# Three pieces later: when a pre-norm attention and MLP kernel loads and squares its other weights

## The chip, the cores and the metric

The kernel runs on one core of a Trainium2 chip. The metric is the device time of one execution in microseconds (us). Before the change the median of three runs is 1648.96 us (1647.39 to 1649.14).

## The reference, cut to what matters

```python
h  = x + softmax_attention(layernorm(x) @ wqkv) @ wo      # 2048 rows, 512 columns, 32 heads of 16
h2 = h + silu(layernorm(h) @ w1) @ w2                     # 512 -> 1792 -> 512
```

All arrays are float32. `wqkv` is 512 x 1536, `wo` 512 x 512, `w1` 512 x 1792 and `w2` 1792 x 512. The reference has no sum of squares of a weight. The kernel needs one for each weight, because it scales weights by powers of two that come from their norms before it splits them into two 16-bit parts.

## The kernel before, in words

**Stages.** The program first computes the first four value tiles and starts the projections (about the first 106 us), goes on with the Q and K projections of the other head groups (to about 200 us), and then runs attention, with the output projection and the MLP of each block of 512 rows woven in. Every engine works off its instructions in program order. SP issues all DMAs, in program order too, so a DMA that has to wait holds up all the DMAs behind it.

**The units of the projections.** The rows come in four blocks (`b` = 0 to 3). The loop at L648 to L691 goes over the blocks, and in a block over units: the K unit and the Q unit of the first head group (`n` = 0, 1, `project_qk`, L521), and, for b = 1 to 3, four V units (`n` = 2 to 5, `project_v`, L545). Unit (b, n) is counted as u = 0, 1 for block 0 and u = 2 + 6(b - 1) + n after it (L654). So (1, 2) is u = 4 and (1, 5) is u = 7. The loop at L716 to L733 follows with three head groups of eight K and Q units, u = 20 to 43; there `n` counts from -4 to 19, with u = n + 24.

**What a unit issues around the change.** A unit begins with `square_rest(u)` (L464). It squares one piece and asks for another:

```python
n = u - 4
if 0 <= n < len(pieces):
    act("activation", staged[n % 2], staged[n % 2], AF.Square, accum_out=rest_sq[:, n:n + 1])
n = u - 2
if 0 <= n < len(pieces):
    dma(staged[n % 2], pieces[n])
```

A piece is 128 x 512 float32, 256 KB, of `w1` (14 of them), `w2` (14) or `wo` (4). Two buffers, `staged`, hold them; both lie in `ks[4]`, so the profile names such a DMA `ks<-in_B_w_dram` (`ks<-in_A_wo_dram` for `wo`) and the square `ks<-ks`. The square is an instruction of ScalarE (ACT), and stands in ACT's order ahead of what the unit itself wants from ACT: the copy of the value tile out of PSUM (`va<-ps_v`, L550), the scaled copy of Q or K (`ks<-ps_qk` and `sh<-ks`, L534 and L535, into `scaled`, also in `ks[4]`), and the copy of turned rows (`xth<-ps_tr`, L209). A DMA into a buffer waits for the square that read it.

A K or Q unit of block 1 or later also has layer-norm work ahead of its product (`stats` and `norm`, by the tables at L645 to L647), GpSimd (POOL) makes the low part `sl`, and two DMAs store the result in `kd` or `qd`. After a Q unit eight DMAs load the block's K rows for the first two attention items (`ks<-kd`, L677; in block 0 eight of Q come with them). After (1, 0) the rows of block 3 are loaded, 1 MB (`load_x(3)`, L689, `ks<-in_A_x_dram`); after (1, 2) and (1, 4) four DMAs each write constant rows (`fixed_rows`, L235, `qs<-fix_q` and `ks<-fix_k`). Row maxima of the scores are woven into the units (`burst`, L393): a matmul into `ps_m`, of which there are five PSUM buffers, and a reduce on VectorE (DVE), `mx<-ps_m`. Products, value tiles and turned rows share three PSUM buffers (`st`). `split_qk` (L500) cuts the next Q or K weights in two: a cast on ACT, a subtraction on DVE, or on POOL in V units; for (1, 5) that is weight 3.

**The values' weights.** `square_values` (L460) squares the raw values' weights, 128 x 2048 elements, in one ACT instruction, and writes the squares over all of `ks[4]`, where nothing reads them. It is issued at L637, after the squares of the Q and K weights and ahead of the copies of the value tiles 1 to 3.

**What uses the sums.** `measure_rest` (L473, called for n = 14) adds the sums up over the partitions with a matmul (`ps_sq`), and `set_factors` (L483, called for n = 16) derives the factors on DVE and POOL. The attention stage uses them.

Of the kernel before, what the change touches and what calls it, by code (L numbers as in the profile page):

```python
# [88 lines left out]
def attention_mlp_kernel(ctx: ExitStack, tc: tile.TileContext, x, wqkv, wo, w1, w2, out):  # L89
# [5 lines left out]
    def mm(*a, **k):  # L95
        tc.keep_in_program_order(nc.tensor.matmul(*a, **k))  # L96
# [12 lines left out]
    def act(fn, *a, **k):  # L109
        pin(getattr(nc.scalar, fn)(*a, **k))  # L110
# [4 lines left out]
    def dma(*a):  # L115
        pin(nc.sync.dma_start(*a))
# [73 lines left out]
    def statistics(rows, scale=1.0):  # L190

        st = small.tile([P, 6], F32, name="st", bufs=5)
        mv = small.tile([P, 2], F32, name="mv", bufs=5)
        rs = small.tile([P, 1], F32, name="rs", bufs=5)
        dve("bn_stats", st, rows)
        dve("bn_aggr", mv, st)
        pool("tensor_scalar", rs, mv[:, 1:2], EPS, scale ** -2, op0=ALU.add, op1=ALU.mult)
        pool("tensor_tensor", rs, rs, expo, ALU.pow)
        return mv, rs

    def normalize(dst, rows, mv, rs, engine="dve"):
        (pool if engine == "pool" else dve)("tensor_scalar", dst, rows, mv[:, 0:1], rs, op0=ALU.subtract, op1=ALU.mult)

    def turn(src, dst_h, dst_l, kind="st"):

        ps = bank("ps_tr", kind).rearrange("p (c n) -> p c n", n=P)
        for c in range(4):
            tr(ps[:, c, :], src[:, c * P:(c + 1) * P], ident)
        act("copy", dst_h, ps)  # L209
        low(dst_l, ps, dst_h)  # L210
# [13 lines left out]
    def load_k(i, k, lo=0, n=S):  # L224
        a, j = HEADS[k]
        h = 4 * (i % 8) + 2 * a + j
        dma(ks[i % RING][64 * j:64 * j + 48, a, lo:lo + n], rows_of_head(kd, h)[:, lo:lo + n])

    def load_q(i, k):
        a, j = HEADS[k]  # L230
        h = 4 * (i % 8) + 2 * a + j
        lo = i // 8 * 512
        dma(qs[i % RING][64 * j:64 * j + 48, a, :], rows_of_head(qd, h)[:, lo:lo + 512])
# [101 lines left out]
    def tick():  # L335
        at["step"] += 1
        for step in [step for step in late if step < at["step"]]:

            finish_rest()
            for i in late.pop(step):  # L340
                place_max(i)
        for fn, a in agenda.pop(at["step"], ()):
            fn(*a)
# [82 lines left out]
    with ExitStack() as pa:  # L426
# [20 lines left out]
        def load_x(b, parts=1):  # L447
            n = 4 // parts
            for t in range(0, 4, n):
                r0 = b * 512 + t * P  # L450
                dma(xts[b][:, t:t + n, :], x[r0:r0 + n * P, :].rearrange("(t p) d -> p t d", p=P))
# [8 lines left out]
        def square_values():  # L460
            act("activation", ks[RING - 1].rearrange("p a n -> p (a n)").bitcast(F32).rearrange(
                "p (c n) -> p c n", n=512), raw_v, AF.Square, accum_out=rest_sq[:, sum(PIECES):])

        def square_rest(u):  # L464

            n = u - 4
            if 0 <= n < len(pieces):
                act("activation", staged[n % 2], staged[n % 2], AF.Square, accum_out=rest_sq[:, n:n + 1])
            n = u - 2
            if 0 <= n < len(pieces):  # L470
                dma(staged[n % 2], pieces[n])

# [21 lines left out]
        def square(n):  # L494
            g, key = divmod(n, 2)
            act("activation", qs[RING - 1].rearrange("p a n -> p (a n)").bitcast(F32).rearrange(
                "p (c n) -> p c n", n=P), raw_qk[key][:, :, g * P:(g + 1) * P],
                AF.Square, accum_out=sq[:, n:n + 1])
# [46 lines left out]
        def project_v(b, t):  # L545
            ps = bank("ps_v")
            weave(product(ps, lambda c: xth[b][:, c, t * P:(t + 1) * P], lambda c: xtl[b][:, c, t * P:(t + 1) * P],
                          lambda c: wv_h[:, c, :], lambda c: wv_l[:, c, :], DC),
                  {k: (lambda n=n: burst(n)) for k, n in BESIDE_V1.items()} if (b, t) == (1, 1) else {})
            act("copy", va[:, 4 * b + t, :, 0:DH], ps.rearrange("p (h d) -> p h d", d=DH))  # L550

        def turn_x(b, t):

            turn(xts[b][:, t, :], xth[b][:, :, t * P:(t + 1) * P], xtl[b][:, :, t * P:(t + 1) * P],
                 "sm" if b == 1 else "st")
# [10 lines left out]
        def columns(t):  # L566
            return slice(t * P, (t + 1) * P)
# [6 lines left out]
        def turn_high(b, t):  # L574
            ps = bank("ps_tr", "sm").rearrange("p (c n) -> p c n", n=P)
            for c in range(4):
                tr(ps[:, c, :], xts[b][:, t, c * P:(c + 1) * P], ident)
            act("copy", xth[b][:, :, columns(t)], ps)
            return ps
# [48 lines left out]
        for t in range(4):  # L628
            for c in range(DC):
                mm(ps_vs[t], xth[0][:, c, columns(t)], wv_l[:, c, :], start=False, stop=False)  # L630
                mm(ps_vs[t], xtl[0][:, c, columns(t)], wv_h[:, c, :], start=False, stop=c == DC - 1)
            act("copy", va[:, t, :, 0:DH], ps_vs[t].rearrange("p (h d) -> p h d", d=DH))
            if t == 0:
                load_x(2)
                for n in (*keys[3:], *range(0, NG, 2)):
                    square(n)
                square_values()  # L637
        turned = [turn_high(1, t) for t in range(2)]
        measure(lambda: normalize(xts[1][:, 3, :], xts[1][:, 3, :], *found.pop(3)))
        for t in range(2):  # L640
# [7 lines left out]
        for b in range(NB):  # L648
            units = [("qk", 1), ("qk", 0)]
            vs = [("v", t) for t in range(4)]  # L650
            found = {}
            for n, (kind, k) in enumerate(units + vs if b else units):
                tick()
                square_rest(2 + 6 * (b - 1) + n if b else n)  # L654
                rows, (stats, norm, turns) = None, ((), (), ())
                if b + 1 < NB:
                    rows = xts[b + 1]
                    stats, norm, turns = (other_ln if b else first_ln)[n]

                def layer_norm():  # L660
                    for t in stats:
                        found[t] = statistics(rows[:, t, :])
                    for t in norm:
                        normalize(rows[:, t, :], rows[:, t, :], *found.pop(t), engine="pool" if kind == "v" else "dve")

                if kind == "v":
                    project_v(b, k)
                else:

                    layer_norm()  # L670
                    project_qk(b, k, scale=b > 0)
                    if k == 0:
                        for i in range(2):
                            for h in range(4):
                                if b == 0:
                                    load_q(i, h)
                                load_k(i, h, b * 512, 512)  # L677
                if b:

                    n_max = BESIDE_V[b - 1][kind == "v"][n - 2 if kind == "v" else n]  # L680
                    burst(n_max, *[bank("ps_m")] * (n_max > 5))
                if kind == "v":
                    layer_norm()
                for t in turns:
                    turn_x(b + 1, t)
                if (b, n) in splits:
                    split_qk(splits.pop((b, n)), "pool" if kind == "v" else "dve")
                if b == 1 and n == 0:
                    load_x(3)  # L689
                if b == 1 and n in (2, 4):  # L690
                    fixed_rows(n // 2 - 1)  # L691
# [24 lines left out]
        for g in range(1, NG // 2):  # L716
            for m, (b, key) in enumerate([(b, 1) for b in range(NB)] + [(b, 0) for b in range(NB)]):
                tick()
                if g == 1 and m < 2:
                    fixed_rows(2 + m)  # L720
                n = 8 * g + m - 12
                square_rest(n + 24)
                if n == 14:
                    measure_rest()
                if n == 16:
                    set_factors()
                beside = {BESIDE_A1[m]: 6} if g == 1 and m < len(BESIDE_A1) else BESIDE_A
                if n >= 18:
                    beside = BESIDE_T[n - 18]
                project_qk(b, 2 * g + key, beside, True, "su" if n % 2 else "st")  # L730
                for load, i, h in loads.get(n, ()):
                    load(i, h)
# [443 lines left out]
    for g in range(groups):  # L1176
# [15 lines left out]
        if i in FIRSTS:  # L1192
            b, n = i // 8 - 1, c - OUTPUT
# [23 lines left out]
        n = maxima(g)  # L1217
# [61 lines left out]
```

## Time and profile before

| | us |
|---|---|
| median of three runs | 1648.96 |
| the profiled execution's own time | 1649.26 |
| its span in the trace | 1647.5 |
| PE busy in the span | 1624.0 (99%) |
| DVE busy | 1439.0 (87%) |
| ACT busy | 1206.6 (73%) |
| POOL busy | 363.5 (22%) |

The profile is of one execution. Its times count from the start of the span. PE is TensorE (PEld its weight loads), DVE VectorE, ACT ScalarE, POOL GpSimd and SP the engine that issues the DMAs. A row of the timeline gives start, duration, engine, line, operation, output and input, and in brackets how long the engine had been idle and what ended that. A row of the chain gives start, duration and what the end of the program waited for at that time. A row of the waits gives the total, the number of times and the longest. A row of the windows gives PE, PEld, DVE, ACT and POOL busy time, and behind them the granted clock of PE (1.00 is full speed), the DMA engines' share and GB/s. L96, L110, L113, L103 and L116 are the helpers for matmuls, ACT, DVE, POOL and SP.

### The profile page before, as it was taken

How to read it: one execution, taken by the hardware profiler on the slowest of the kernel's cores; microseconds unless marked ns; L12 is line 12 of the kernel's file. 1: busy time of each engine (PE TensorE's matmuls, PEld its weight loads, DVE VectorE, ACT ScalarE, POOL GpSimd, SP SyncE). 2: the span in 40 equal slices, each digit the busy share in tenths (PEclk: the TensorE clock that was granted, in tenths of full speed). 3: DMA queues.
4: the chain of work that ended last, by engine and by line, in shares of the span. 5: the costliest groups of instructions: out<-in, count | busy, mean ns of one | idle time of the engine just before them, and what ended most of it. 6: DMA issues, size and time to landing. Idle time of an engine off the chain costs nothing.

```text
span 1647.5 us, 28474 instructions
## 1 busy us (share of the span) xinstructions
PE 1624.0 (99%) x10553; PEld 516.1 (31%) x10553; DVE 1439.0 (87%) x2385; ACT 1206.6 (73%) x2391; POOL 363.5 (22%) x594
## 2 busy tenths in 40 slices
PE   9899999999999999999999999999999999999999
PEld 7566522222223322222223322222233322222254
DVE  7799999999999989999999989999988969999431
ACT  5445599999972169999972169999972179999732
POOL 4323354544421001121121001121121001111100
PEclk9999999999999999999999999999999999999999
DMA  5657344333432211111232211112132211100222
GB/s 192 170 142 220 100 96 121 99 107 107 117 76 85 71 51 32 34 36 49 54 76 85 70 51 32 33 36 53 51 77 90 65 50 32 36 12 21 72 81 73
DMA packets 100951, 125.91 MB, mean 76 GB/s; under 512 B 24144, under 2 KB 61072, under 8 KB 100812
## 3 DMA queue, kind: packets, MB, share of 16 engines
q1 hardware_dynamic: 100812, 124.10, 27.1%
q8 instruction: 82, 1.34, 0.3%
q14 instruction: 57, 0.47, 0.1%
HBM read 93.45 MB, written 24.63 MB: 72 GB/s over the span
## 4 chain that ended last, share of the span: by engine, by line
PE 79%; DVE 14%; ACT 4%; DMA 2%; issue 1%; POOL 0%; SPq 0%; DVEq 0%; ACTq 0%
PE pv L96 32%; PE ps_s L96 21%; DVE mx L271 11%; PE ps_m L96 10%; PE ps_qk L96 5%; PE ps_acc L96 4%; PE ps_w L96 3%; ACT pt L110 3%; PE ps_wo L96 2%; PE ps_v L96 2%; DVE gh L113 1%; DMA ks<-in_B_w_dram 1%; PE ps_tr L99 1%; DVE ot L113 0%; DVE pvs L113 0%
## 5 line engine op out<-in xcount | busy, mean ns | idle before, releaser
L271 DVE TENSOR_REDUCE mx<-ps_m 128x1 f32<-128x512 f32 x2011 | 1260.5, 683 | 68.1 <-PE ps_m L96 36.4
L110 ACT ACTIVATE pt<-ps_s 128x512 f32<-128x512 f32 x2048 | 1010.4, 608 | 30.0 <-PE ps_m L96 17.8
L96 PE MATMUL pv<-pt,va 128*17 128x512 f32 x4096 | 537.6, 598 | 0.9
L96 PE MATMUL ps_s<-qs,ks 64*128 64x512 f16 x2048 | 532.6, 379 | 2.0 <-ACT pt L110 0.5
L96 PE MATMUL ps_m<-ks,qs 48*128 48x512 f16 x2011 | 513.6, 381 | 9.0 <-DVE mx L271 6.1
L96 PEld LDWEIGHTS <-ks 64*128 64x128 f16 x2048 | 150.3, 95 | 550.0 <-issue 437.1
L110 ACT ACTIVATE g<-pv,factors 128x512 f32<-128x512 f32 x39 | 26.8, 688 | 217.5 <-PE pv L96 217.5
L96 PE MATMUL ps_acc<-w,gh 128*128 128x512 f16 x672 | 161.2, 380 | 0.0
L103 POOL TENSOR_TENSOR ri<-rc,minus 128x16 f32<-128x16 f32 x31 | 90.9, 2932 | 282.0 <-DMA rc<-dn 282.0
L96 PEld LDWEIGHTS <-qs 48*128 48x128 f16 x2048 | 119.6, 94 | 76.1 <-issue 70.1
L96 PEld LDWEIGHTS pv<-pt,va 128*17 128x17 f32 x4096 | 69.0, 95 | 215.3 <-issue 202.7
L103 POOL TENSOR_TENSOR mx<-mx 128x32 f32<-128x32 f32 x34 | 8.6, 254 | 403.5 <-DVE mx L271 402.0
L113 DVE SCALAR_TENSOR_TENSOR gh<-g,factors,gh 128x512 f16<-128x512 f32 x56 | 41.7, 745 | 63.7 <-ACT gh L110 63.7
L96 PEld LDWEIGHTS <-w 128*128 128x128 f16 x708 | 65.2, 98 | 93.6 <-issue 29.1
L96 PE MATMUL pv<-hth,w 128*128 128x512 f16 x312 | 92.9, 379 | 0.0
L96 PEld LDWEIGHTS <-gh 128*128 128x128 f16 x672 | 59.2, 98 | 95.1 <-issue 32.4
L110 ACT ACTIVATE ks<-ps_qk,qk_s 128x512 f32<-128x512 f32 x30 | 20.7, 689 | 53.3 <-PE ps_qk L96 45.7
L96 PE MATMUL pv<-htl,w 128*128 128x512 f16 x156 | 59.5, 381 | 0.0
L103 POOL TENSOR_SCALAR nm<-nm 128x16 f32<-128x16 f32 (+1 forms) x50 | 13.1, 261 | 198.7 <-DVE nm L282 195.7
L96 PE MATMUL ps_qk<-xth,wqk_h 128*128 128x512 f32 x128 | 53.6, 419 | 0.6 <-ACT va L110 0.6
L96 PE MATMUL ps_qk<-xth,wqk_l 128*128 128x512 f32 x128 | 50.7, 396 | 0.0
L103 POOL TENSOR_TENSOR sl<-ks,sh 128x512 f16<-128x512 f32 x30 | 34.8, 1161 | 70.4 <-ACT sh L110 56.9
(134 smaller groups left out, 1002.8 us busy)
## 6 DMA issues: line engine op xcount, KB each, us to landing
ks<-kd SPq DMA_DIRECT2D x120, 192.0 KB
w<-w1d SPq DMA_DIRECT2D x56, 256.0 KB
w<-w2d SPq DMA_DIRECT2D x56, 256.0 KB
ks<-in_B_w_dram SPq DMA_DIRECT2D x28, 256.0 KB
w<-in_B_w_dram SPq DMA_DIRECT2D x28, 256.0 KB
qs<-qd SPq DMA_DIRECT2D x128, 48.0 KB
kd<-sh SPq DMA_DIRECT2D x16, 256.0 KB
qd<-sh SPq DMA_DIRECT2D x16, 256.0 KB
```

Of the source, the lines that this page charges most:

```text
L96: tc.keep_in_program_order(nc.tensor.matmul(*a, **k))
L99: tc.keep_in_program_order(nc.tensor.transpose(*a))
L103: tc.keep_in_program_order(getattr(nc.gpsimd, op)(*a, **k))
L110: pin(getattr(nc.scalar, fn)(*a, **k))
L113: pin(getattr(nc.vector, fn)(*a, **k))
L271: pin(nc.vector.tensor_reduce(mx[piece][:, j, a % n, qt, kb:kb + 1], ps, axis=AX.X, op=ALU.max))
```

## The change

```diff
         def square_rest(u):
-            n = u - 4
+            n = u - 7
             if 0 <= n < len(pieces):
                 act("activation", staged[n % 2], staged[n % 2], AF.Square, accum_out=rest_sq[:, n:n + 1])
-            n = u - 2
+            n = u - 5
             if 0 <= n < len(pieces):
                 dma(staged[n % 2], pieces[n])
...
                 for n in (*keys[3:], *range(0, NG, 2)):
                     square(n)
-                square_values()
...
                 for t in turns:
                     turn_x(b + 1, t)
+                if (b, n) == (0, 1):
+                    square_values()
                 if (b, n) in splits:
                     split_qk(splits.pop((b, n)), "pool" if kind == "v" else "dve")
...
                 square_rest(n + 24)
-                if n == 14:
+                if n == 15:
                     measure_rest()
-                if n == 16:
+                if n == 17:
                     set_factors()
```

Each of the 32 pieces is asked for and squared three units later: the loads move from u = 2 to 33 to u = 5 to 36, the squares from u = 4 to 35 to u = 7 to 38. The values' weights are squared in unit (0, 1), after its product and ahead of the split of weight 4, instead of ahead of block 0. `measure_rest` and `set_factors` come one unit later. No instruction is added or dropped.

## The prediction

> **What bounds the kernel now.** I read the waits of the whole span first, then the chain of the first 115 us, then the timelines of ACT, SP and PE and the windows. TensorE is busy 99% of the span, and the work behind the projections runs in a fixed order at that pace, so what counts is a stall ahead of it. The waits name one: ACT, waiting for pieces of `w1`.
>
> ```profile
> ACT ks L110 <- DMA ks<-in_B_w_dram: 23.4, 10, 5.4
> ```
>
> The four squares of u = 4 to 7 hold most of it, by the tile view of the pieces' DMAs in 30 to 70 us, and ACT's timeline has the first and the last of the four:
>
> ```profile
>   ACT ks L110: 17.7, 4
> ```
>
> ```profile
> 43.04 0.63 ACT L110 ACTIVATE ks<-ks 128x512 f32<-128x512 f32 x1 [5.38 <-DMA ks<-in_B_w_dram]
> ...
> 60.37 0.63 ACT L110 ACTIVATE ks<-ks 128x512 f32<-128x512 f32 x1 [3.33 <-DMA ks<-in_B_w_dram]
> ```
>
> The copies that free PSUM stand behind each square, so the wait is on the chain of work that ended last:
>
> ```profile
> 51.50 3.83 DMA ks<-in_B_w_dram
> ...
> 55.65 4.70 DMA ks<-in_B_w_dram
> ...
> 64.97 2.39 DVE mx L271 x4
> ...
> 72.45 3.00 PE ps_v L96 x12
> ...
> 76.57 2.74 PE ps_v L96 x12
> ...
> 80.43 2.74 PE ps_v L96 x12
> ```
>
> The reader is to see that the last of the four waits sets the time. The piece that unit (1, 5) squares is issued at 55.65 and lands 4.70 later, at T = 60.35. From there the chain runs through the square, the copy of the value tile, the cast of weight 3, POOL's low part, the layer norm and DVE's maxima (64.97, T + 4.6) until V unit (2, 1) starts on PE at 72.45, which is T + 12.1. Two units on, a unit takes 80.43 - 76.57 = 3.86 us, and PE hardly stands still any more. So the change is worth what it moves T, unless something else becomes later than T.
>
> **The change, part by part.**
>
> *The loads and squares that leave.* Units u = 2, 3, 4 issue no piece, u = 4, 5, 6 square none, and their waits, 17.7 - 3.33 = 14.4 us, go. What is late next is the fourth: u = 5 still asks for a piece, now piece 0, and u = 7 still squares it. The new T hangs on when SP reaches u = 5.
>
> ```profile
> 40.07 0.42 SPq L116 DMA_DIRECT2D ks<-in_B_w_dram  x1
> ...
> 41.58 0.46 SPq L116 DMA_DIRECT2D ks<-in_A_x_dram  x1
> ...
> 44.71 6.70 SPq L116 DMA_DIRECT2D ks<-kd  x8
> 51.50 0.37 SPq L116 DMA_DIRECT2D ks<-in_B_w_dram  x1
> ...
> 57.26 0.60 SPq L116 DMA_DIRECT2D qs<-fix_q  x1
> ...
> 59.20 1.08 SPq L116 DMA_DIRECT2D ks<-fix_k  x1
> ```
>
> ```profile
> SPq L116 <- DMA ks<-in_A_x_dram: 2.6, 1, 2.6
> ```
>
> ```profile
> 49.31 0.30 SPq L116 DMA_DIRECT2D ks<-kd  x1
> ```
>
> SP has hardly a free moment from 40.07 to 60.28 (59.20 + 1.08). In the middle of the eight K loads it waits 2.6 us until block 3's rows, issued at 41.58, have landed; it goes on at 49.31, 7.73 after that issue. The steps in the changed kernel:
>
> 1. All SP work up to there is 0.58 sooner (next part), and piece 0's slot, about 0.5 to the next issue, is gone: block 3's rows go out at 41.58 - 0.58 - 0.5 = 40.5.
> 2. They have 256 KB less ahead of them and 256 KB less behind. At the 360 GB/s that the DMA engines move in the window from 49 to 50 below, 256 KB are 0.7 us. So they land 7.73 (nothing gained) to 6.3 (both gained) after the issue; I take 6.9, most of the first and little of the second: 47.4.
> 3. From 49.31 to the next piece at 51.50 were 2.2 us, some of it waiting behind the piece of u = 3. I take 1.6 (1.4 to 2.2): 49.0.
> 4. The four DMAs of constant rows: 60.28 - 57.26 = 3.0 for the second set; the first lay between 51.50 and 55.65, less 0.5 for the piece at 51.50: 3.6. I take 3.0: piece 0 goes out at 52.0.
> 5. It lands 4.70 later, like the piece at 55.65, or 3.83 later, like the one at 51.50 with no constant rows just ahead. The rows are just ahead here, but less else is in flight; I take 4.0.
>
> Together T' = 56.0, and 60.35 - 56.0 = **4.3 us gained**. With all low ends T' is 46.8 + 1.4 + 3.0 + 3.8 = 55.0; with all high ends 48.2 + 2.2 + 3.6 + 4.7 = 58.7. So the gain is 1.7 to 5.4 by this sum.
>
> *PE may not be later than that.* It starts V unit (1, 3) at 38.15.
>
> ```profile
> 38.15 0.48 PE L96 MATMUL ps_v<-wv_h,xth 128*128 128x512 f32 x1
> ...
> 46.09 1.78 PE L96 MATMUL ps_m<-ks,qs 48*128 48x512 f16 x3 [3.87 <-DVE mx L271]
> ```
>
> With the next part's delay it starts by 39.5. Five units, to the end of the product of (2, 1), take at most 5 x 3.86, so PE is there by 58.8 (rather 57.5, since three of them turn no rows). The maxima that it needs there come at T' + 4.6 = 60.6. PE waits for them some 2 to 3 us, and T' + 12.1 stands. The 3.87 us gap of PE at 46.09 goes.
>
> *The square of the values' weights* costs the same wherever it stands.
>
> ```profile
> 20.15 1.92 ACT L110 ACTIVATE ks<-va 128x2048 f32<-128x2048 f32 x1
> ```
>
> ```profile
> 22.68 0.50 PE L96 MATMUL ps_qk<-xth,wqk_h 128*128 128x512 f32 x1 [0.58 <-ACT va L110]
> ```
>
> At its old place PE's first K product waits 0.58 behind it; that is gained, for SP's stores and loads too. At its new place the split of weight 4 is queued behind it on ACT, then that split's low part on DVE, and behind this the layer norm whose rows PE turns before V unit (1, 2). So up to 1.92 - 0.58 = 1.34 us come back on PE. It is hidden by the wait for T', and the K and Q stores of block 1 are not SP's limit. Without this cover it costs up to 1.34.
>
> *The late end.* Squares come into u = 36, 37, 38 and loads into u = 34, 35, 36; the sum's matmul comes at n = 15, the factors at n = 17.
>
> ```profile
> 172.05 0.69 ACT L110 ACTIVATE ks<-ps_qk,qk_s 128x512 f32<-128x512 f32 x1 [2.40 <-PE ps_qk L96]
> ```
>
> ```profile
> 175.53 0.30 PE L96 MATMUL ps_sq<-qs,ones 128*128 128x33 f32 x2
> ```
>
> This is the scaled copy of u = 36, with ACT idle for 2.40 before it: a square of 0.63, with the short read of its sum behind it, fits in. The matmul moves from 175.53 to about 179.3, a unit on. The last square runs as soon as the copies of u = 37 are done, near 177.1, and ends before 178, so PE has some 1.4 us to spare. SP has two issues a unit besides there. The factors' small DVE and POOL instructions are as many as before and stand one unit later, still two units ahead of the attention stage, where their first use is some steps in. I take nothing; if a piece came late, the price would be that lateness less 1.4.
>
> Sum: 0 + 4.3 + 0 = 4.3. The profiled execution took 1649.26, 1.76 more than its span, and would take 1645.0. It lies 0.3 above the median of the three runs, 1648.96, for which I forecast **1644.7**.
>
> **The rivals.**
>
> *Half clock in the new gap.* PE's gap of 3.87 had an aftermath in the granted clock:
>
> ```profile
> 46.00:47.00 1.00, 0.89 (x2) 0.20 (x2) 1.00 (x3) 0.00 (x0) 0.00 (x0) 0.54 0.76 152
> ...
> 49.00:50.00 1.00, 1.00 (x4) 0.71 (x4) 1.00 (x3) 0.04 (x1) 0.00 (x0) 0.50 1.03 360
> ...
> 52.00:53.00 1.00, 1.00 (x4) 0.73 (x4) 0.36 (x1) 0.00 (x0) 0.00 (x0) 0.55 0.66 131
> ```
>
> The clock was half from 46.0 to 52.9, 6.8 us. Before the change this is free, since the next piece is later still. The gap that I expect in the changed kernel, 2 to 3 us, lies in unit (2, 1), and behind it nothing else waits: of 6.8 us at half clock the first 2.4 run at DVE's pace (the maxima of the row at 64.97), and the other 4.4 lose half, 2.2 us. The gain would be 4.3 - 2.2 = 2.1: 1646.9. For it speaks the one gap in the trace, against it that the new gap is shorter. [...]
>
> *Slower: the half clock stays.* The same mechanism at the same place, with a price that grows by half of the time it lasts. The clock came back in the trace only while PE ran a whole V unit without a pause. In units (2, 1) to (2, 5) PE stops for DVE's reductions now and then, which could keep it down. It eats up the gain from 2.4 + 2 x 4.3 = 11 us on; at 20 us it costs (20 - 2.4) / 2 = 8.8, and the time is 1648.96 - 4.3 + 8.8 = 1653.5. Against it speaks that the one fall in the trace lasted 6.8 us and that a unit is mostly PE's own work.
>
> *The wait only moves.* That is, T' comes out near 59.3, because SP's K loads and constant rows, not the pieces, fill the DMA engines: then the gain is the two issue slots of 0.5 us ahead of it, 1.0: 1648.0. For it speaks that SP is busy nearly without a break and that every wait in the trace was followed by another; against it, that three pieces and the 2.6 us wait behind them are taken out of just this stretch.
>
> *The wait goes further.* If block 3's rows land before the K loads need them, these start at 44.71 - 1.1 = 43.6, take 6.70 - 2.6 = 4.1, the constant rows 3.0 and the piece 3.8: T' = 54.5, a gain of 5.8: 1643.2.
>
> **How the numbers follow.** I give the forecast 0.55, the short half clock 0.14, the lasting one 0.06, the wait that only moves 0.14, the wait that goes further 0.11. A measurement of this kernel can tell about 0.2% from no change, 3.3 us; faster by more means under 1645.7. The forecast's own range, 1643.6 to 1647.3, lies under that with some 0.46 of its 0.55, and all of the 0.11 does: 0.57. The short half clock (0.14), the moved wait (0.14) and the rest of the forecast (0.09) make 0.37 for no difference. Slower is the lasting half clock, 0.06. The range runs from 1642.6, somewhat under the wait that goes further, to 1648.8, above the one that only moves; it leaves out the lasting half clock and the tails.
>
> **What would show it right or wrong.** Right, if ACT waits for pieces not four times but once in block 1, before its square in unit (1, 5), with the piece landing at 55 to 57; if V unit (2, 1) starts some 12.1 later, near 68.1 instead of 72.45; if the granted clock stays at 1.00 from 46 to 53; if PE's first K product starts near 22.1; and if, from that V unit on, every stage to the end is sooner by the same 4.3. Wrong, if the landing moves by less than 1.7, if a window near 61 to 68 shows a clock of 0.50, or if the sum's matmul waits for ACT's last square near 175.

## The result and the profile after

The changed kernel takes 1646.33 us (median of 20 runs, 1644.63 to 1647.60) and the kernel before 1648.95 us (20 runs, 1647.39 to 1650.18) on the same chip. The ratio is 0.9982, with a 95% interval of 0.9976 to 0.9989: a gain of 2.6 us, 0.16%, where 4.3 were forecast. That is inside the range, and inside the 0.2% that the prediction called no difference. The profiled execution took 1647.2 us, with a span of 1645.4. One execution each of e2 and e8, below, took 3098.81 and 4209.76 us; the times given for these two kernels are medians of their other executions.

Three views answer first. The waits of 20 to 115 us, of the kernel before and then of the changed one:

```profile
ACT ks L110 <- DMA ks<-in_B_w_dram: 20.2, 6, 5.4
```

```profile
ACT ks L110 <- DMA ks<-in_B_w_dram: 11.0, 3, 7.7
```

The timelines of ACT and of SP, of the changed kernel:

```profile
56.40 0.63 ACT L110 ACTIVATE ks<-ks 128x512 f32<-128x512 f32 x1 [7.72 <-DMA ks<-in_B_w_dram]
```

```profile
40.70 0.40 SPq L116 DMA_DIRECT2D ks<-in_A_x_dram  x1
...
42.46 7.49 SPq L116 DMA_DIRECT2D ks<-kd  x8
50.00 0.76 SPq L116 DMA_DIRECT2D qs<-fix_q  x1
...
52.82 1.62 SPq L116 DMA_DIRECT2D ks<-in_B_w_dram  x2
```

The waits for pieces in this stretch fell from 20.2 us to 11.0. The large one is the wait forecast, before the square of unit (1, 5), and the piece has landed by 56.4 (T = 60.35 before, forecast 56.0). SP's steps come as forecast, each late by 0.2 to 1.0: block 3's rows at 40.70 (40.5), the end of the K loads at 49.95 (49.0), piece 0 out at 52.82 (52.0). So the square is 3.97 us sooner. V unit (2, 1) is only 2.51 sooner. The chain of work that ended last, PE's timeline and the windows of the same kernel:

```profile
64.44 4.38 PE ps_v L96 x12
...
69.94 2.79 PE ps_v L96 x12
...
73.85 2.74 PE ps_v L96 x12
```

```profile
61.61 0.58 PE L96 MATMUL ps_m<-ks,qs 48*128 48x512 f16 x1 [3.52 <-DVE mx L271]
```

```profile
60.00:61.00 1.00, 0.00 (x0) 0.00 (x0) 0.58 (x2) 0.00 (x0) 0.83 (x3) 1.00 1.02 376
61.00:62.00 1.00, 0.39 (x1) 0.10 (x1) 1.00 (x2) 0.21 (x1) 1.00 (x2) 0.50 0.87 300
...
67.00:68.00 1.00, 1.00 (x4) 0.77 (x4) 1.00 (x3) 0.00 (x0) 1.00 (x2) 0.59 0.00 0
```

PE stands still for 3.52 us in unit (2, 1); a stop of 2 to 3 us was forecast there. Behind it the granted clock is 0.50 from 61.0 to 67.8 (0.59 in the last row means half speed for 0.82 of that microsecond). A value product that takes 2.74 takes 4.38, and V unit (2, 1) starts at 69.94. With T' for the new landing (56.37), it would have started at T' + 12.1 = 68.47, as far behind the landing as in the kernel before: 1.47 us lost.

More is lost at the end of the projections. From V unit (2, 2) to the first product behind unit n = 18 the kernel before takes 195.54 - 76.57 = 118.97 and the changed one 193.51 - 73.85 = 119.66. The two chains there, first of the kernel before, then of the changed one:

```profile
188.47 1.11 PE ps_m L96 x6
...
192.60 0.17 ACT mt L110
...
192.81 0.37 PE ps_s L96
...
195.54 1.13 PE ps_qk L96 x4
```

```profile
183.02 3.07 DVE mx L271 x5
186.09 1.06 DVE factors L113 x2
...
187.56 2.98 DVE mx L271 x5
...
190.58 0.40 PE ps_m L96 x2
...
193.51 1.12 PE ps_qk L96 x4
```

Before, PE is the pace there, up to its wait for ACT's `mt`. Afterwards DVE is: the maxima and the factors between them run without a break, and PE waits for them.

The profiled execution adds up: 3.98 from the landing, less 1.47 for the clock, plus 0.21 between V units (2, 1) and (2, 2), less 0.69 at the end, is 2.03; the spans differ by 2.1. So from there on hardly anything changes.

### The profile page after: what moved, and what is told of

It is laid out like the page before. It is cut to its first block, busy times and chain, and to the rows that moved or that the text cites. A ratio compares the mean times of both kernels' runs of the same rounds, so it can differ in the third digit from the quotient of the medians.

```text
span 1645.4 us, 28475 instructions
## 1 busy us (share of the span) xinstructions
PE 1623.2 (99%) x10553; PEld 516.2 (31%) x10553; DVE 1439.6 (87%) x2385; ACT 1207.1 (73%) x2391; POOL 362.5 (22%) x594
## 4 chain that ended last, share of the span: by engine, by line
PE 79%; DVE 14%; ACT 3%; issue 1%; DMA 1%; POOL 0%; SPq 0%; DVEq 0%; ACTq 0%; POOLq 0%
PE pv L96 32%; PE ps_s L96 21%; DVE mx L271 11%; PE ps_m L96 10%; PE ps_qk L96 5%; PE ps_acc L96 4%; PE ps_w L96 3%; ACT pt L110 3%; PE ps_v L96 2%; PE ps_wo L96 2%; DVE gh L113 1%; PE ps_tr L99 1%; DMA qd<-sh 0%; DVE ot L113 0%; DVE pvs L113 0%
```

## The experiments

Three questions: does the half clock explain the 1.47, which part of the change brings the gain, and what costs 0.69 at the end. Every kernel ran in five rounds against the kernel before (1649.46, 1649.08 and 1648.69 us in the three groups of runs). The last column is the stretch from V unit (2, 2) to the first product behind n = 18, in the profile.

| kernel | time, us | ratio to before (95%) | V unit (2, 1) | stretch |
|---|---|---|---|---|
| before | 1648.95 | 1 | 72.45 | 118.97 |
| after | 1646.33 | 0.9982 (0.9976 to 0.9989) | 69.94 | 119.66 |
| e1_filler | 1644.97 | 0.9972 (0.9961 to 0.9982) | 67.69 | 119.65 |
| e3_pieces_only | 1647.15 | 0.9987 (0.9978 to 0.9995) | 69.73 | 119.64 |
| e2_values_only | 1649.26 | 1.0001 (0.9991 to 1.0010) | 71.98 | 118.96 |
| e5_rows_later | 1641.08 | 0.9951 (0.9938 to 0.9965) | 63.48 | 120.06 |
| e6_one_more_unit | 1641.14 | 0.9950 (0.9937 to 0.9964) | 63.16 | 119.51 |
| e8_unit_and_rows | 1639.86 | 0.9945 (0.9932 to 0.9957) | 62.81 | 119.51 |
| e4_factors16 | 1645.77 | 0.9979 (0.9970 to 0.9988) | 68.22 | 119.55 |
| e7_rows_factors | 1640.88 | 0.9951 (0.9939 to 0.9964) | 63.54 | 119.93 |
| e9_late_end_only | 1649.95 | 1.0007 (0.9998 to 1.0016) | 72.82 | 119.68 |
| e10_other_bank | 1646.40 | 0.9987 (0.9978 to 0.9996) | 68.04 | 120.10 |
| e11_bank_rows | 1641.95 | 0.9958 (0.9945 to 0.9972) | 63.48 | 120.56 |
| e12_bank_filler | 1645.72 | 0.9985 (0.9976 to 0.9994) | 67.42 | 120.16 |

My theory is that the gain is what the landing moves, less the half clock, less a price of the late end. The rivals stand in the expectations.

### The half clock

**e1_filler** keeps PE at work in the gap: 14 matmuls behind the product of unit (2, 1), into a spare bank.

```diff
                     project_qk(b, k, scale=b > 0)
+                    if (b, n) == (2, 1):
+                        ps = bank("ps_i", "sm")
+                        for _ in range(14):
+                            mm(ps, wqk_h[:, 0, :P], xth[b][:, 0, :], start=True, stop=True)
```

> The changed kernel with 14 matmuls of 128x512 added on TensorE in unit (2, 1), behind its product and ahead of its maxima; their result is used by nothing. Theory A (the clock at half from 61 to 67.8 eats part of the gain): the matmuls fill the gap from 57.7 to 61.6, the granted clock stays at 1.00, V unit (2, 1) starts 12.1 after the landing of piece 0, near 68.5 instead of 69.9, and the time falls by 1.4 to about 1644.9. Theory B (the landing alone sets the time, the clock is free as it was before the change): no difference to 1646.3, and V unit (2, 1) still starts near 69.9. Worse than 1646.3 would mean that the added matmuls themselves get in the way.

Windows, chain and ACT's timeline of this kernel:

```profile
61.00:62.00 1.00, 0.78 (x4) 0.28 (x4) 1.00 (x3) 0.90 (x3) 0.76 (x1) 1.00 0.29 99
```

```profile
67.69 3.03 PE ps_v L96 x12
```

```profile
55.62 0.63 ACT L110 ACTIVATE ks<-ks 128x512 f32<-128x512 f32 x1 [6.73 <-DMA ks<-in_B_w_dram]
```

The piece still comes late and ACT still waits 6.73, but the clock is 1.00 here and in every row from 60 to 68, and V unit (2, 1) starts 67.69 - 55.60 = 12.1 behind the landing, as before the change. So the half clock and nothing else of the gap was the price. The added matmuls stand behind the landing on PE and can't move it, yet in this execution it was 0.8 sooner than in the profiled one of the changed kernel; e4 and e10, which are alike up to there, have their squares at 55.35 and 55.19. The landing varies by over 1 us from one execution to the next, and the forecast of 56.0 lies within.

The price varies too. V unit (2, 1) is 13.6 behind the landing in the changed kernel, 13.2 in e3, and 12.9 in e4 and e10: it cost 1.5, 1.1 and 0.8 us. The time of e1 is 1.4 below the changed kernel's, measured in another group of runs; the intervals of the two ratios overlap. A second pair was measured together: e12, with the added matmuls, is 0.7 faster in the median than e10, without them, and its V unit (2, 1) starts 67.42 - 55.33 = 12.1 behind the landing.

### Which part brings the gain

**e3_pieces_only** is the changed kernel with `square_values` at its old place, **e2_values_only** the kernel before with `square_values` at its new place.

```diff
                 for n in (*keys[3:], *range(0, NG, 2)):
                     square(n)
+                square_values()
...
-                if (b, n) == (0, 1):
-                    square_values()
```

> The changed kernel with the square of the values' weights back at its old place. Theory A (the pieces carry the gain): the landing of piece 0 comes some 0.4 later, near 56.8, the gap of TensorE grows to about 5 us since TensorE loses no time to that square in block 1, the clock falls to half in it, and the time is 1646.6 to 1647.2. Theory B (the two parts carry about equal shares): about 1647.8.

```diff
                     square(n)
-                square_values()
...
                     turn_x(b + 1, t)
+                if (b, n) == (0, 1):
+                    square_values()
```

> The kernel before with one part of the change alone: the square of the values' weights in unit (0, 1), the pieces, the sum and the factors where they were. Theory A (this part only takes the wait of TensorE's first K product away, which brings SP and with it the landing of the last late piece forward by about 0.4): V unit (2, 1) starts near 72.0, the time falls by 0.4 to about 1648.6. Theory B (its new place delays the layer norm of block 1 and TensorE, and this counts): slower than before by up to 1.1.

The pieces alone come out 0.8 above the changed kernel, in a run of its own whose interval overlaps with it; the profiles are alike, with V unit (2, 1) at 69.73 and 69.94. PE's gap is longer there (5.00 us, since PE gets to it sooner), with a clock of 0.50 behind it again, in every row from 61 to 67. The square alone makes no difference that can be measured. Its trace shows 0.47 us at V unit (2, 1), from the SP work that is sooner:

```profile
59.89 0.63 ACT L110 ACTIVATE ks<-ks 128x512 f32<-128x512 f32 x1 [3.26 <-DMA ks<-in_B_w_dram]
```

```profile
71.98 3.01 PE ps_v L96 x12
```

Half a microsecond is under what the times can tell, so whether it is worth that stays open. That it costs 1.1 is not borne out.

### The wait for piece 0, further

**e5_rows_later** loads the first two sets of constant rows, which stand ahead of piece 0 at SP, in block 2. **e6_one_more_unit** loads and squares one more unit later. **e8_unit_and_rows** has both edits.

```diff
-                if b == 1 and n in (2, 4):
+                if b == 2 and n in (2, 4):
                     fixed_rows(n // 2 - 1)
```

> The changed kernel with the two sets of constant rows written in block 2 (after units (2, 2) and (2, 4)) instead of block 1. Theory A (the time hangs on the landing of piece 0 and this on SP's way to unit (1, 3)): piece 0 goes out at about 50.0 instead of 52.8 and lands near 53 instead of 56.4, TensorE has almost no gap in unit (2, 1) and keeps its clock, V unit (2, 1) starts near 65 instead of 69.9, and the time is about 1641.5. Theory B (DMA traffic, not SP's order, sets the landing): it lands near 56 and the time stays at 1646.3. If the rows hold up later pieces as much, up to 2 us of the gain go again.

```diff
-            n = u - 7
+            n = u - 8
...
-            n = u - 5
+            n = u - 6
...
-                if n == 15:
+                if n == 16:
                     measure_rest()
```

> The changed kernel with pieces one more unit later: loads from u = 6, squares from u = 8, the sum measured at n = 16, the factors at n = 17. Theory A (what the late piece holds up is the chain square, value copy, cast of weight 3, GpSimd's low part, layer norm, DVE): the piece lands about as late as now, near 56, but its square stands behind the value copy and the cast, so the layer norm of unit (2, 0) runs at about 55 and V unit (2, 1) starts near 63; the time is about 1639.7. Theory B (any wait of ACT for a piece costs its length, wherever it stands): the wait before the square is as long or longer and the time stays within 1 us of 1646.3.

> The changed kernel with the pieces one more unit later and the constant rows in block 2. Theory A (behind unit (2, 0) DVE sets the pace once no piece holds up the layer norm): V unit (2, 1) starts near 63.2 as with one more unit alone, and the time stays at 1641.1. Theory B (the wait for the pieces still counts): the pieces land some 3 us sooner and the time falls under 1640.

The squares that waited, and the chain, of e5 and then of e6:

```profile
51.64 0.63 ACT L110 ACTIVATE ks<-ks 128x512 f32<-128x512 f32 x1 [3.40 <-DMA ks<-in_B_w_dram]
```

```profile
63.48 2.73 PE ps_v L96 x12
```

```profile
55.12 0.63 ACT L110 ACTIVATE ks<-ks 128x512 f32<-128x512 f32 x1 [3.46 <-DMA ks<-in_B_w_dram]
59.49 0.63 ACT L110 ACTIVATE ks<-ks 128x512 f32<-128x512 f32 x1 [2.42 <-DMA ks<-in_B_w_dram]
```

```profile
63.16 3.00 PE ps_v L96 x12
```

Each gains 5 us more than the changed kernel, and in neither does the clock fall (1.00 in every row from 56 to 68). In e5 V unit (2, 1) is 1.5 sooner than expected. In e6 ACT waits for two pieces, 3.46 and 2.42, and yet V unit (2, 1) starts at 63.16, as expected: a unit later, nothing that PE needs soon is queued behind the wait. Here the place of a wait counts for more than its length. The time of e6 is 1.4 above the one expected; the longer stretch at the end (119.51) accounts for 0.5 of that. Together the two edits bring 1.2 us more than either, where one theory had nothing and the other at least 1.1. The piece is there before its square, at 51.44, and ACT doesn't wait for it, but V unit (2, 1) moves by only 0.35 against e6, and the spans of the two profiled executions differ by 0.5. So the trace shows less than half of the 1.2; where the rest comes from stays open. At 1639.86 this is the fastest kernel here, 0.9945 (0.9932 to 0.9957) of the kernel before.

The stretch of e5 is 0.4 longer than that of the changed kernel. This lies ahead of the sum's matmul (103.28 us from V unit (2, 2) to it, against 102.89), and not in the late end.

### The late end

The first suspects were DVE's factors. DVE's and POOL's timelines of the changed kernel, and DVE's of the kernel before:

```profile
186.01 1.13 DVE L113 TENSOR_SCALAR factors<-qs 128x3 f32<-128x3 f32 x2
```

```profile
185.91 1.15 POOL L103 TENSOR_TENSOR sl<-ks,sh 128x512 f16<-128x512 f32 x1 [1.12 <-ACT sh L110]
```

```profile
184.96 0.21 DVE L113 TENSOR_SCALAR factors<-qs 128x3 f32<-128x3 f32 x2
```

Two tiny instructions (of 128 x 3 and, merged into the same row, 128 x 1 elements) that took 0.21 take 1.13. One unit later they come while POOL makes a low part (185.91 to 187.06); they are done at 187.14. **e4_factors16** puts the factors back at n = 16, and **e7_rows_factors** does so in e5.

```diff
-                if n == 17:
+                if n == 16:
                     set_factors()
```

> The changed kernel with the factors set in unit n = 16, as before the change, and the sum still measured at n = 15. Theory A (0.7 us of the gain are lost at the end of the projections because DVE's first two factor instructions ran 1.1 instead of 0.2 us beside a GpSimd subtraction): those two take about 0.2 us again, and the time falls by 0.7 to about 1645.6. Theory B (the late loss is something else, the squares in units 36 to 38): no difference to 1646.3.

> The changed kernel with the constant rows in block 2 and the factors at n = 16. Theory A (the late landing with its half clock and the slow factor instructions are separate losses): the time is 1641.1 - 0.7 = 1640.4, and DVE's first two factor instructions take about 0.2 us. Theory B (they overlap): 1641.1 as with the rows alone.

By its time alone e4 looks like a success: 0.6 below the changed kernel where 0.7 were expected. The trace says otherwise. The two instructions do take 0.21 again, but the stretch is 119.55, only 0.11 shorter. The profiled execution of e4 is faster for other reasons, a landing 1.05 sooner and a half clock of 3.4 instead of 6.8 us. And e7 gains nothing that can be measured over e5. So the theory of the factors falls as the whole cause. The late factors alone, with the sum at its old place, were not run. Another wait takes its place; the chain of e4 names it:

```profile
184.87 0.37 PE ps_m L96
...
188.42 0.50 ACT pt L110
...
188.96 0.37 PE ps_m L96
...
191.68 1.13 PE ps_qk L96 x4
```

In the kernel before, PE goes on at 192.81 when ACT has copied `mt`. Here the third matmul for maxima of unit n = 18 waits 0.5 longer, for the exponentials `pt`. The two kernels issue the same instructions in that unit; but the sum's matmul takes one of the six PSUM buffers that go around there, and in the compiled order this matmul now waits for ACT, where before the change it followed the scores' matmul without a pause. **e9_late_end_only** tests whether the late sum and factors are the cause at all, with nothing else of the change. **e10_other_bank** takes the sum's buffer from the other pool and has the factors at n = 16, with which the matmul no longer waits for `pt`. **e11_bank_rows** and **e12_bank_filler** are e5 and e1 with these two edits.

```diff
-                if n == 14:
+                if n == 15:
                     measure_rest()
-                if n == 16:
+                if n == 17:
                     set_factors()
```

> The kernel before with the late end of the change alone: the sum's matmul at n = 15 and the factors at n = 17; loads and squares stay where they were. Theory A (the later sum and factors themselves cost the 0.7 us that the changed kernel loses between n = 16 and the attention stage): V unit (2, 1) starts at 72.45 as before, and from the end of n = 18 on everything is 0.7 later, 196.2 where the kernel before has 195.54; the time is 0.7 above the kernel before, 1649.7 to 1649.9. Theory B (the 0.7 comes from the late squares of pieces or the late loads, which are not in this kernel): nothing is later, 195.5, and the time is that of the kernel before.

```diff
             n = sum(PIECES)
-            ps = bank("ps_sq", "sm")
+            ps = bank("ps_sq", "st")
...
-                if n == 17:
+                if n == 16:
                     set_factors()
```

> The changed kernel with the sum's matmul, still at n = 15, into the other pool of PSUM banks, and the factors back at n = 16. In the changed kernel and in the two with only the factors moved, the third maximum's scores of unit n = 18 wait for ACT's exponentials; in the kernel before they wait for DVE's maxima. With this edit they wait for DVE again. Theory A (the late 0.7 is two things, DVE's 1.13 us for the factors beside POOL and the bank that waits for ACT): from V unit (2, 1) to behind n = 18 it takes as long as before, so what is gained at V unit (2, 1) is still there at 195.54 to within 0.15, and the time is 0.6 below the changed kernel, 1645.6 to 1645.8. Theory B (DVE does the sum's reductions one unit later and has no time to catch up): 0.5 or more is still lost there, and the time is 1646.2.

> The kernel before this one with the first two sets of constant rows loaded in block 2 as well. Theory A: V unit (2, 1) at 63.5 as with the rows alone, nothing lost at n = 17 and 18, so 187.4 becomes 186.7 and the time is 0.6 below the kernel with the rows alone (1641.1): 1640.4. Theory B (with DVE and ACT so close behind one another another wait takes the place, as with rows and factors): 1640.9 to 1641.1.

> The kernel with the sum in the other pool of banks and the factors at n = 16, with the 14 extra matmuls in unit (2, 1) whose result isn't used. Both terms that the prediction had at nothing are taken away. Theory A: they add up, 1.4 for the clock and 0.6 for the late end: 1644.3 to 1644.5, V unit (2, 1) at 67.7, and the 4.8 us gained there are all there behind n = 18. Theory B (they overlap): 1645.0, no better than the extra matmuls alone.

The chain of e9 behind n = 18, and that of e10:

```profile
188.98 1.06 DVE factors L113 x2
...
196.40 1.13 PE ps_qk L96 x4
```

```profile
174.85 0.70 ACT ks L110
...
175.59 0.41 PE ps_sq L96 x2
...
184.95 1.09 PE ps_m L96 x6
...
189.06 0.17 ACT mt L110
...
189.27 0.37 PE ps_s L96
...
192.00 1.12 PE ps_qk L96 x4
```

e9 is the kernel before up to V unit (2, 2). In this execution that starts at 76.72, 0.15 later than there, since the landing was 0.4 sooner and the clock fell (more on this at the end). From there it takes 119.68: the late sum and factors, and not the late squares or loads, cost 0.71. e2 is the counterpart, with the old end and 118.96. In the times e9 is 1.3 slower with an interval that takes in no difference, so it is the trace that shows it.

In e10 the end goes as in the kernel before: the six matmuls take 1.09 (1.11 before), then `mt` is what PE waits for. From the sixth of these to 192.00 it is 5.96, as before the change (195.54 - 189.58), where e4 has 191.68 - 185.24 = 6.44. So with the other buffer the 0.5 is gone. But the edit has a price of its own that I had not seen: the other pool has a single buffer, which still holds the product of the unit before, and the sum's matmul waits until ACT has made the scaled copy of it (175.59). This costs 1.1, more than it saves. So e10, e11 and e12 end no faster, or slower, than the kernels without the edit, and the expected times were not reached in any of the three. A caution: PE's wait at 175 also gives DVE time to catch up, so that the buffer alone is the 0.5 is shown only beside that wait.

## Why the prediction was right and wrong

**Right: the chain and the landing.** The late piece set the time, three of the four waits went, the fourth stayed at the square of unit (1, 5), the clock stayed at 1.00 from 46 to 53, and the landing moved from 60.35 to 56.4, by 3.97 of the 4.3 forecast (55.2 to 56.4 over the executions). The largest error is in the K loads, which ended at 49.95, not at 49.0. SP's waits of the changed kernel from 40 to 56 us say why:

```profile
SPq L116 <- DMA ks<-in_A_x_dram: 2.0, 1, 2.0
SPq L116 <- DMA qd<-sh: 1.9, 1, 1.9
```

The wait for block 3's rows is 2.0 instead of 2.6, but the one for the store of Q is 1.9, where it was 0.4. The constant rows took 2.8 (52.82 - 50.00, forecast 3.0) and the piece 3.55 (56.37 - 52.82, forecast 4.0), which gives most of it back: the landing is 0.4 late.

**Wrong: "PE waits for them some 2 to 3 us, and T' + 12.1 stands."** This is the step that failed. PE waited 3.52, and the clock fell, so V unit (2, 1) came at T' + 13.6. The wait was longer than forecast because DVE's first maximum, which begins at T' + 4.6 as forecast (60.96), has to end before PE goes on (61.57), and because the landing itself was 0.4 late. A clock of 0.50 between 61 and 68 was one of the prediction's own signs of being wrong. It was also its first rival, with a price of 2.2 us and a chance of 0.14; the price was 1.47 here, and 0.8 to 1.1 in other executions. The first part of the half clock is indeed free, since DVE is the pace (the matmuls for maxima from 61.61 on start 0.60 apart, as they do from 65.62 on at full clock in the kernel before), and only V unit (2, 0), 4.38 instead of 2.74, and the matmuls around it pay. That a gap of 2 to 3 us would cost nothing was my own estimate, which no run had shown. The runs disagree with it: in e4 the clock fell behind a gap of 2.92, and in e9 behind one of 1.50. PE's timelines of e4 and then of e9:

```profile
60.58 0.37 PE L96 MATMUL ps_m<-ks,qs 48*128 48x512 f16 x1 [2.92 <-DVE mx L271]
```

```profile
65.18 0.37 PE L96 MATMUL ps_m<-ks,qs 48*128 48x512 f16 x1 [1.50 <-DVE mx L271]
```

The windows of e4:

```profile
62.00:63.00 1.00, 1.00 (x6) 0.93 (x6) 0.96 (x3) 0.83 (x3) 0.00 (x0) 0.69 0.44 133
...
65.00:66.00 1.00, 1.00 (x4) 0.76 (x3) 1.00 (x2) 0.00 (x0) 1.00 (x2) 0.60 0.04 8
```

In e4 it was half from 62.38 to 65.80, 3.4 us, half of the 6.8 in the changed kernel's profile. It was 3.4 us in e9 too (67.46 to 70.88, by the clock in its rows) and 6.8 in the kernel before. What sets these lengths no run here shows.

**Wrong: the late end, "I take nothing."** No square and no wait of the sum's matmul cost anything there, as argued. The place of the sum and the factors costs 0.69. I had counted the instructions ("as many as before") and PE's slack, not what they meet: DVE's maxima and factors leave it no gap from 183.02 to 190.54, so a delay on DVE isn't caught up there; two of its instructions took 0.9 us more beside one of POOL's (1.13 instead of 0.21); and the sum changes which buffer the last unit waits for. These overlap: with the factors back at their old place, the sum alone costs nearly as much (0.58, e4).

**Small: the front.** The first K product started at 22.30 instead of 22.68, 0.38 sooner and not 0.58.

```profile
22.30 0.48 PE L96 MATMUL ps_qk<-xth,wqk_h 128*128 128x512 f32 x1
```

The two terms together, 1.47 + 0.69 = 2.16, are more than the whole difference between the forecast and the median (1646.33 - 1644.7 = 1.6); the profiled execution lies 0.9 above the median. That the time fell inside the range is in part luck: the range had been drawn around the rivals too, and with two terms put at nothing the result lies nearer to the first rival (1646.9) than to the forecast.

**The other rivals.** The half clock did not last (slower, 1653.5), the wait did not only move (1648.0), and it did not go further by itself (1643.2); for that the constant rows had to go out of its way (e5).

## What to carry to other kernels

Before a wait is shortened, ask what the gap that remains does to TensorE's clock: filling it can win back what the clock takes (in e1 V unit (2, 1) came 12.1 us behind the landing instead of 13.6), and moving the wait to where nothing needed soon is queued behind it can be worth more than shortening it (e6). Small instructions that are moved are not free because they are as many as before; look at which engine has no slack at the new place, what runs beside them (0.21 us became 1.13 here), and which shared buffer they take. When an edit moves the time as expected, check in the trace that it did so at the place it was meant for: e4 did not.

## What the runs showed of the hardware

In e9 the granted clock fell to 0.50 behind a stop of 1.50 us, with short matmuls (0.37 us) at DVE's pace behind it. In the kernel before PE stood idle for much of 64 to 67, its longest stop 0.85 us, and the clock stayed at 1.00; in e9, the same program up to there, that stop was the longest and the clock fell at 67.5. One execution of each can't tell whether the length decided it or when it came. The windows:

```profile
65.00:66.00 1.00, 0.37 (x1) 0.09 (x1) 1.00 (x2) 0.00 (x0) 1.00 (x2) 1.00 0.71 241
```

```profile
67.00:68.00 1.00, 1.00 (x7) 0.86 (x5) 0.97 (x3) 1.00 (x3) 0.17 (x1) 0.73 0.72 172
68.00:69.00 1.00, 1.00 (x3) 0.79 (x3) 0.96 (x4) 0.58 (x2) 0.83 (x3) 0.50 0.81 296
```

Two DVE instructions, on 128 x 3 and 128 x 1 elements, took 1.13 instead of 0.21 us beside a POOL instruction of 1.15 that had begun 0.10 sooner, and ended 0.08 behind it. They took as long in e3, e5 and e6 (1.14); with the factors at n = 16, where POOL runs instructions of 0.2 us at that time, they took 0.21. Why they take longer there no run here shows.
